# A searched order for the first stage of attention and FFN: q and k loads ahead of v, and x copied to SBUF before it is split

## The chip, the cores and the metric

One core of a Trainium2 chip runs the whole program. The metric is device time in microseconds of one launch; the median of the runs shown is 946.67 us before the change.

## What is computed

Attention with 8 heads over 8 sequences of 576 positions, then a feed-forward layer. Heads 0 to 3 see a window of 32 positions, heads 4 to 7 a window of 128 with dilation 4. Cut to what matters:

```python
scores = q @ k.T / 8            # masked: window of 32, or 128 with dilation 4
attn = softmax(scores)
x = (attn @ v)                  # heads side by side: 4608 tokens x 512
h = x @ w_in                    # 512 x 2048
out = gelu(h) @ w_out           # 2048 x 512
```

All arrays are float32. Q and K come with a larger spread than V.

## The kernel before

The 4608 tokens are cut into 16 chunks of 288 (half a sequence each). A chunk c has four pairs of heads, p = 0 and 1 for the plain window, 2 and 3 for the dilated one. This text writes S(c,p) for the scores of a pair on PE (`scores`, L310), AV(c,p) for its product with v (`av`, L395 or L411), h(c,f) for one of 16 slices of the first FFN product (`ffn_h`, L445, 12 matmuls) and o(c,f) for its part of the second (`ffn_o`, L459, 12 matmuls, 3 for each of four output slices d).

A pair goes: load of q and k (one DMA, L262) and of v (L269); S into two PSUM banks; minimum and mask on DVE (`lowest`, L322); exp on ACT (`softmax`, L331); sums, reciprocal (L352, L354); the division on DVE (L361) or, for chunks 1 and 2, on POOL (L358); a transpose on DVE (`turn`, L371); AV into PSUM (tile px, one buffer for chunks 0 and 1); and `xout`, which splits x into a high part xh (ACT, L431) and the rest xl (DVE, L434), both read from PSUM. The FFN needs x of all four pairs: each h(c,f) multiplies two parts of a weight slice with xh and one with xl. g = gelu(h) is split in the same way (L449, L452, L454).

The 32 weight slices (w_in and w_out by turns, w0 to w31) come as 64-bit words and are turned into a high and a low part on DVE and ACT (`w_rest`, `w_top`, `w_exp`, `w_high`, `w_low`). A slice is loaded once (L185), or twice, the second time shifted by two bytes (L189, tile mid_w), for the slices from TWICE[0] to TWICE[1]-1. With the second load one DVE operation (L216) stands where two stand otherwise (L220, L222).

Chunks 0 to 2 and all weights are the first stage. Its order comes from the class `Plan`: every job is a generator that tells which engine its next step takes and for how long; `run` always takes the step with the lowest key of start time and rank, and the instructions are emitted in that order. The constants ahead of the class (LATE, KAPPA, R_A and so on) are the ranks and delays. Jobs also wait in the plan for buffers (`rings`): `wo` (18 buffers: raw weights, second loads, finished w_out slices, q/k and v of chunks 0 and 1), `raw` (5 buffers: cv of the weights, and q and k from chunk 2 on), `m` (4 PSUM banks for scores and h), `px`. All loads are issued by one queue, SP, in the planned order, and a load that waits for a buffer holds all behind it. From chunk 3 on the order is a table of positions (A_SC and so on), in which attention of chunk c+1 lies between the FFN products of chunk c.

Lines that matter here: `attention_jobs` L501 to L541 adds a pair's jobs, `weight_jobs` L543 to L559 those of a weight slice, `store` L479 copies a finished output slice and writes it out (L177 on ACT or L179 on DVE).

```python
LATE, LATE_PE, COLD = 0.3, 0.3, 38
KAPPA, AHEAD = 0.00011, 6
TWICE = (1, 20)
add("load", load(s), [("begun", ("load",) + j) for j in last], [ring], delay=2.2)
```

Of the kernel before, what the change touches and what calls it, by code (L numbers as in the profile page):

```python
# [7 lines left out]
F32 = mybir.dt.float32  # L8
F32R = mybir.dt.float32r
# [8 lines left out]
P = 128  # L18
HALF = S // 2
NCH = B * 2  # L20
NPAIR = H // 2
NF = DFF // P
NC = DM // P
# [13 lines left out]

LATE, LATE_PE, COLD = 0.3, 0.3, 38  # L40
KAPPA, AHEAD = 0.00011, 6
R_ATT, R_P = (0, 680, 660), -52
R_F = 152
R_A = {"load": 172, "v": -214, "scores": 30,
       "exp": 84, "norm": 88, "t": -122, "av": -410, "x": -184, "less": -68, "sums": -20, "low": -110}
R_W, R_WL = -360, -404
R_H, R_O, R_E, R_O1 = 492, 1336, 908, 608


class Plan:  # L50
# [67 lines left out]

N_EARLY = 2

TWICE = (1, 20)


def at_once(gen):
# [10 lines left out]
def attn_ffn(ctx: ExitStack, tc: tile.TileContext, qk_p, qk_d, v_p0, v_d0, v_p, v_d, w_in, w_out, outT):  # L135
    nc = tc.nc
# [4 lines left out]
    xpool = ctx.enter_context(tc.tile_pool(name="xpool", bufs=NC))  # L141
    work = ctx.enter_context(tc.tile_pool(name="work", bufs=2))
# [150 lines left out]
    def scores(s, banks=None):  # L293

        yield {"PE": 0.75}
        if banks is None:
            s.sc = [ps_m.tile([P, 512], F32, tag="m", name="ps_sc")[:, 0:2 * KB * NU] for _ in range(2)]
        else:
            s.sc = [banks[:, h, s.p % 2 * 2 * KB * NU:(s.p % 2 + 1) * 2 * KB * NU] for h in range(2)]
        for u in range(NU):  # L300
            for r in groups(s, u):
                if s.across:
                    q0 = (4 * u + r if u < 2 else 8) * KB
                    k0 = HALF + q0
# [74 lines left out]
    def av(s, banks=None):  # L379
# [24 lines left out]
        for u in range(NU):  # L404
            b = min(KB, n - u * KB)
            for j in range(2):
                for r in sorted((r for r in groups(s, u) if r % 2 == j), reverse=s.across and s.nine > 0):
                    px, r0, _ = s.px[-1] if r >= s.px[-1][1] else s.px[0]
                    rows = slice(r // 2 * 64, r // 2 * 64 + 64)
                    for h in range(2):  # L410
                        nc.tensor.matmul(px[h * D:(h + 1) * D, r - r0, u * KB:u * KB + b],  # L411
                                         s.v[rows, u, j, h * D:(h + 1) * D], s.t[rows, 2 * u + h, j, 0:b],
                                         start=True, stop=True)

    def xout(s):
        for i, (px, r0, r1) in enumerate(s.px):
            yield {"ACT": 0.46 if len(s.px) == 1 else 0.34}
            if i == 0:
                if s.c == 1:
                    s.x = s.of["x"][:, s.p, 0], s.of["x"][:, s.p, 1]  # L420
                else:
                    s.x = tuple(xpool.tile([P, HALF], F32R, tag=n, name=n) for n in ("xh", "xl"))
            if s.across:
                two = [x[:, 0:8 * KB].rearrange("p (u r b) -> p r u b", u=2, r=4) for x in s.x]
                put = [(px[:, :, 0:2 * KB].rearrange("p r (u b) -> p r u b", u=2), two),
                       (px[:, s.nine, 2 * KB:], [x[:, 8 * KB:] for x in s.x])]
            else:
                put = [(px, [x.rearrange("p (r i) -> p r i" if s.plain else "p (i r) -> p r i", r=s.nr)[:, r0:r1]
                             for x in s.x])]
            for y, (h, l) in put:  # L430
                nc.scalar.copy(h, y)  # L431
            yield {"DVE": 0.48 if len(s.px) == 1 else 0.3}
            for y, (h, l) in put:
                nc.vector.tensor_sub(l, y, h)  # L434
# [54 lines left out]
    g0, g1, x1 = {}, {}, {}  # L489
# [11 lines left out]
    def attention_jobs(plan, c, prev, gate):  # L501

        for p in range(NPAIR):
            s, k, rank = xs[c][p], (c, p), R_ATT[c] + R_P * p

            def add(name, gen, after, take=(), give=(), delay=0.15):
                plan.add((name,) + k, gen, after, take, give, rank + R_A[name], delay)
            last, ring = [] if prev is None else [prev], "wo" if c < 2 else "raw"
            add("load", load(s), [("begun", ("load",) + j) for j in last], [ring], delay=2.2)
            v = ("v",) + k if c < 2 else ("v", c)  # L510
            if c < 2:
                add("v", load_v(s), [("begun", ("load",) + k)] + [("begun", ("v",) + j) for j in last], [ring], delay=2.2)
# [12 lines left out]
            add("scores", scores(s), [("load",) + k] + [("scores",) + j for j in last], ["m", "m"], [ring], 1.5)
            chained("low", NU, lowest, lambda b: [("scores",) + k] + ([("begun", ("t", 1, NPAIR - 1))] if c == 2 else []),
                    ["sm"], ["m", "m"])
            if c < 2:
                chained("exp", NU, softmax, lambda b: [all_of("low", NU)[0] if b == NU - 1 else ("low", b) + k] + gate)
                add("norm", norm(s), all_of("exp", NU))  # L530
            else:
                add("less", less(s), all_of("low", NU))
                add("exp", wide(s), [("less",) + k] + gate)
                add("sums", sums(s), [("exp",) + k])
                add("norm", norm(s), [("sums",) + k])
            add("t", turn(s), [("norm",) + k], ["sm"], ["sm"])
            own = ["px"] if c < 2 else ["m", "m"]
            add("av", av(s), [("t",) + k, v], own, ["sm"] + ([ring] if c < 2 else []), 1.5 if c < 2 else 0.3)
            add("x", xout(s), [("av",) + k] + ([("x1",)] if c == 1 else [("h", 0, NF - 1)] if c == 2 else []), give=own)
            prev = k  # L540
        return prev  # L541

    def weight_jobs(plan, i):  # L543

        s, f = {"twice": TWICE[0] <= i < TWICE[1]}, i // 2
        dst, src = (wouts, w_out) if i % 2 else (wins, w_in)
        rank = R_W + R_F * f + R_O * (i % 2)
        own = ["wo"] if i % 2 else []
# [21 lines left out]
    def take_o():  # L570
        yield {"": 0.0}
        pools["o"] = upper_banks("ps_o", NC)
    plan.add(("banks",), take_o(), [("x", c, p) for c in range(2) for p in range(NPAIR)], [], ["o"] * NC, -100)
    ps0, ps1 = [], {}
    for f in range(NF):
        rank = R_W + R_F * f
        for c, gs in ((0, g0), (1, g1)):
# [29 lines left out]
    steps, banks = [], {}  # L607
# [26 lines left out]
    at = 0  # L634
# [96 lines left out]
```

## Time and profile before

| | |
|---|---|
| runs | 945.33, 946.67, 946.92 us; median 946.67 |
| the profiled execution | 945.82 us, of it the span of the instructions 944.0 us |
| PE matmuls busy | 916.4 us (97%), 11632 instructions |
| PE weight loads busy | 898.6 us (95%) |
| DVE busy | 500.2 us (53%) |
| ACT busy | 435.4 us (46%) |
| POOL busy | 21.0 us (2%) |
| DMA | 83.69 MB, mean 89 GB/s; in the first tenth of the span 261 to 405 GB/s |
| chain that ended last | PE 96%, DMA 1%, issue 1%, DVE 1% |

The profiled execution took 1.8 us beside its span and lies 0.85 us under the median of the runs. PE is busy in all of the 40 slices but the first two and the last. A float32 matmul of the scores or of AV runs as two instructions, so 18 of them stand as x36 in the trace; an h or o matmul is one.

### The profile page before, as it was taken

Reading aid. Unit: us, or ns where it says so; the run is one execution under the profiler, and the core shown is the slowest. Engines: PE = TensorE matmul, PEld = TensorE weight load, DVE = VectorE, ACT = ScalarE, POOL = GpSimd, SP = SyncE. Lnnn points to the kernel's source line nnn. Section 1 sums busy time; section 2 is a strip of 40 time slices with the busy share of each in tenths; the row PEclk is TensorE's granted clock in tenths of the full one; section 3 lists DMA queues with packets and bytes.
Section 4 is the critical chain, followed back from the end, with each engine's and each line's share of the span. In section 5 each row is a group of like instructions: output and inputs, shape, how many; then the busy total and the mean of one; then the engine's idle time right before and its main releaser. Section 6 shows DMA issues by size and latency. Waiting matters only on the chain.

```text
span 944.0 us, 27638 instructions
## 1 busy us (share of the span) xinstructions
PE 916.4 (97%) x11632; PEld 898.6 (95%) x11632; DVE 500.2 (53%) x1957; ACT 435.4 (46%) x1398; POOL 21.0 (2%) x64
## 2 busy tenths in 40 slices
PE   4599999999999999999999999999999999999998
PEld 3499999999999999999999999999999999999998
DVE  6889974364635446354454635446354454635420
ACT  5535453634536245363634546255363634546240
POOL 1400020000000000000000000000000000000000
PEclk9999999999999999999999999999999999999999
DMA  9987233022040401204022040401204022040000
GB/s 319 405 297 261 92 126 137 4 78 75 8 145 8 132 17 51 103 8 145 2 82 71 8 146 8 138 9 60 93 8 145 2 86 68 13 139 8 21 1 26
DMA packets 34988, 83.69 MB, mean 89 GB/s; under 512 B 3888, under 2 KB 12080, under 8 KB 34864
## 3 DMA queue, kind: packets, MB, share of 16 engines
q1 hardware_dynamic: 34864, 81.93, 25.3%
q8 instruction: 91, 1.49, 0.7%
q14 instruction: 33, 0.27, 0.1%
HBM read 72.47 MB, written 9.44 MB: 87 GB/s over the span
## 4 chain that ended last, share of the span: by engine, by line
PE 96%; DMA 1%; issue 1%; DVE 1%; ACT 0%; SPq 0%
PE ps_h L445 44%; PE ps_o L459 44%; PE px_a L411 4%; PE ps_a L310 3%; DMA raw_qk<-qk_d 1%; PE px L395 1%; PE ps_sc L310 1%; DMA raw_w<-w_in 0%; DVE sm L322 0%; PE px L411 0%; DVE cv L199 0%; DVE sm L361 0%; ACT sm L331 0%; DVE cv L197 0%; DVE win L232 0%
## 5 line engine op out<-in xcount | busy, mean ns | idle before, releaser
L459 PE MATMUL ps_o<-g,wout 128*128 128x288 f32 x3072 | 420.1, 296 | 0.0
L459 PEld LDWEIGHTS ps_o<-g,wout 128*128 128x128 f32 x3072 | 409.7, 188 | 0.9
L445 PE MATMUL ps_h<-xh,win 128*128 128x288 f32 x1920 | 388.7, 297 | 0.0
L445 PEld LDWEIGHTS ps_h<-xh,win 128*128 128x128 f32 x1920 | 308.2, 188 | 2.8
L445 PE MATMUL ps_h<-xl,win 128*128 128x288 f32 x960 | 284.0, 296 | 0.0
L454 DVE TENSOR_TENSOR g<-gf,g 128x288 fp32r<-128x288 f32 x256 | 117.0, 457 | 259.2 <-ACT g L452 259.0
L449 ACT ACTIVATE gf<-ps_h 128x288 f32<-128x288 f32 x256 | 105.2, 411 | 297.6 <-PE ps_h L445 297.5
L445 PEld LDWEIGHTS ps_h<-xl,win 128*128 128x128 f32 x960 | 181.0, 189 | 0.0
L331 ACT ACTIVATE sm<-sm,st 128x64 f32<-128x64 f32 (+1 forms) x360 | 120.2, 335 | 12.5 <-DVE st L322 11.4
L452 ACT CAST g<-gf 128x288 fp32r<-128x288 f32 x256 | 111.0, 434 | 7.9
L431 ACT CAST xh<-px_a 128x256 fp32r<-128x256 f32 (+1 forms) x78 | 29.5, 413 | 132.7 <-PE px_a L411 84.8
L376 DVE STREAM_TRANSPOSE turned<-sm 32x192 f32<-32x192 f32 (+2 forms) x248 | 81.3, 328 | 6.2
L179 DVE COPY o_sb<-ps_o 128x288 f32<-128x288 f32 x58 | 26.4, 456 | 83.3 <-PE ps_o L459 82.4
L331 ACT ACTIVATION_READ_ACCUMULATOR sm<-sm,st 128x1 f32 (+1 forms) x360 | 67.2, 187 | 0.0
L434 DVE TENSOR_TENSOR xl<-px_a,xh 128x256 fp32r<-128x256 f32 (+1 forms) x78 | 31.3, 429 | 37.5 <-ACT xh L431 37.1
L322 DVE CUSTOM_DVE_ANT_0 sm<-ps_a,masks 128x64 f32<-128x64 f32 (+1 forms) x312 | 48.0, 216 | 0.6
L371 DVE STREAM_TRANSPOSE turned<-sm 128x256 f32<-128x256 f32 (+2 forms) x90 | 41.1, 457 | 9.0 <-POOL sm L358 4.2
L411 PEld LDWEIGHTS px_a<-turned,v_all 64*64 64x64 f32 x2184 | 35.6, 135 | 4.3 <-issue 4.3
L411 PE MATMUL px_a<-turned,v_all 64*64 64x32 f32 (+1 forms) x2184 | 38.2, 216 | 0.0
L361 DVE TENSOR_TENSOR sm<-sm,st 128x256 f32<-128x256 f32 (+2 forms) x82 | 35.1, 428 | 2.8
L352 DVE TENSOR_SCALAR st<-st 128x4 f32<-128x4 f32 (+2 forms) x90 | 14.2, 160 | 31.0 <-ACT sm L331 30.1
L310 PE MATMUL ps_sc<-raw_qk 64*32 64x64 f32 x504 | 12.3, 294 | 18.8 <-issue 8.4
(40 smaller groups left out, 392.8 us busy)
## 6 DMA issues: line engine op xcount, KB each, us to landing
raw_qk<-qk_d SPq DMA_DIRECT2D x32, 364.0 KB, 5.4
v_all<-v_p SPq DMA_DIRECT2D x28, 384.0 KB, 3.8
v_all<-v_d SPq DMA_DIRECT2D x28, 384.0 KB, 5.4
raw_qk<-qk_p SPq DMA_DIRECT2D x32, 304.0 KB, 4.2
outT<-o_sb SPq DMA_DIRECT2D x64, 144.0 KB, 1.8
raw_w<-w_in SPq DMA_DIRECT2D x16, 512.0 KB, 6.1
raw_w<-w_out SPq DMA_DIRECT2D x16, 512.0 KB, 5.7
mid_w<-w_out SPq DMA_DIRECT2D x10, 511.5 KB, 8.0
```

Of the source, the lines that this page charges most:

```text
L310: nc.tensor.matmul(s.sc[h][32 * r:32 * r + 32, u * 2 * KB:(u + 1) * 2 * KB], x[:, q0:q0 + 32], x[:, k0:k0 + 2 * KB], start=True, stop=True)
L322: nc.vector.tensor_tensor_reduce(out=s.sm[rs, i], in0=s.sc[h][rs, cols], in1=mask_of(s, u), scale=-SCALE, scalar=3.0e38, op0=ALU.add, op1= ...
L331: nc.scalar.activation(t, t, AF.Exp, bias=s.st[rs, 0, i:i + 1], scale=-1.0, accum_out=s.st[rs, 1, i:i + 1])
L361: nc.vector.tensor_mul(t, t, st.unsqueeze(2).broadcast_to((rs.stop - rs.start, 2 * (u1 - u0), 2 * KB)))
L371: nc.vector.transpose(s.t[rs, i].rearrange("p i j b -> p (i j b)"), s.sm[rs, i].rearrange("p i k -> p (i k)"))
L376: nc.vector.transpose(s.t[32 * to:32 * to + 32, i, r % 2], s.sm[32 * r:32 * r + 32, i, j * KB:(j + 1) * KB])
L411: nc.tensor.matmul(px[h * D:(h + 1) * D, r - r0, u * KB:u * KB + b], s.v[rows, u, j, h * D:(h + 1) * D], s.t[rows, 2 * u + h, j, 0:b], sta ...
L445: nc.tensor.matmul(ps, wins[f][:, t, cc * P:(cc + 1) * P], xx, start=(n == 0), stop=(n == 3 * NC - 1))
L449: nc.scalar.activation(gf, ps, AF.Gelu)
L452: nc.scalar.copy(g[:, 0], gf)
L454: nc.vector.tensor_sub(g[:, 1], gf, g[:, 0])
L459: nc.tensor.matmul(ps, wouts[f][:, t, d * P:(d + 1) * P], gs[f][:, u], start=(f == 0 and n == 0), stop=(f == NF - 1 and n == 2))
```

## The change

Three things, all in the first stage. (1) The constants of the plan are others. (2) The load of q and k of pair number n of chunks 0 and 1 may begin once the scores of pair n-5 have begun (NEXT), and no longer in step with v; those of chunk 2 wait for the low part of weight slice 1 (LATER). (3) For chunks 0 and 1 (VIA) x is copied by ACT from PSUM to an SBUF tile x32 (`xcopy`), and `xsplit` makes xh from it on ACT and xl on DVE; px is free after the copy. TWICE ends at 28 in place of 20, so slices 20 to 27 are loaded twice too.

```diff
-LATE, LATE_PE, COLD = 0.3, 0.3, 38
-KAPPA, AHEAD = 0.00011, 6
+LATE, LATE_PE, COLD = 0.4, 0.55, 38
+KAPPA, AHEAD = 6.4e-05, 6
...
+NEXT, LATER = 5, 1
+
+VIA = (0, 1)
+
-TWICE = (1, 20)
+TWICE = (1, 28)
...
+    def xcopy(s):
+        yield {"ACT": 0.46}
+        s.x32 = work.tile([P, HALF], F32, tag="go", name="x32", bufs=3)
+        nc.scalar.copy(by_group(s, s.x32, 0, s.nr), s.px[0][0])
+
+    def xsplit(s):
+        yield {"ACT": 0.34}
+        new_x(s)
+        nc.scalar.copy(s.x[0], s.x32)
+        yield {"DVE": 0.37}
+        nc.vector.tensor_sub(s.x[1], s.x32, s.x[0])
...
-            add("load", load(s), [("begun", ("load",) + j) for j in last], [ring], delay=2.2)
+            gates, at = [], NPAIR * c + p - NEXT
+            if c == 2:
+                gates = [("wlow", LATER)]
+            elif at >= 0:
+                gates = [("begun", ("scores", at // NPAIR, at % NPAIR))]
+            add("load", load(s), [("begun", ("load",) + j) for j in last] + gates, [ring], delay=2.2)
...
-            add("x", xout(s), [("av",) + k] + ([("x1",)] if c == 1 else [("h", 0, NF - 1)] if c == 2 else []), give=own)
+            if c in VIA:
+                add("xc", xcopy(s), [("av",) + k], ["go"], own)
+                add("x", xsplit(s), [("xc",) + k] + ([("x1",)] if c == 1 else []), give=["go"])
+            else:
+                add("x", xout(s), [("av",) + k] + ([("x1",)] if c == 1 else [("h", 0, NF - 1)] if c == 2 else []), give=own)
```

What the new constants do to the order is seen in the built programs. First PE, from the scores S(1,2) to the first h. L310 and L314 are scores, L395 and L399 AV, L445 and L466 h; a scores row holds 18 or 24 matmuls for each pair, an AV three rows for each pair. Before:

```order
13 L310 MATMUL ps_sc<-raw_qk 32x64 x48
14 L395 MATMUL px<-turned,v_sb 64x64 x8
15 L395 MATMUL px<-turned,v_sb 64x32 x16
16 L395 MATMUL px<-turned,v_sb 64x64 x8
17 L310 MATMUL ps_sc<-raw_qk 32x64 x18
18 L395 MATMUL px<-turned,v_sb 64x64 x6
19 L395 MATMUL px<-turned,v_sb 64x32 x12
20 L395 MATMUL px<-turned,v_sb 64x64 x6
21 L445 MATMUL ps_h<-xh,win_116 128x288 x2
```

And now:

```order
13 L314 MATMUL ps_sc<-raw_qk 32x64 x24
14 L399 MATMUL px<-turned,v_sb 64x64 x8
15 L399 MATMUL px<-turned,v_sb 64x32 x16
16 L399 MATMUL px<-turned,v_sb 64x64 x8
17 L314 MATMUL ps_sc<-raw_qk 32x64 x24
18 L399 MATMUL px<-turned,v_sb 64x64 x6
19 L399 MATMUL px<-turned,v_sb 64x32 x12
20 L399 MATMUL px<-turned,v_sb 64x64 x6
21 L314 MATMUL ps_sc<-raw_qk 32x64 x18
22 L399 MATMUL px<-turned,v_sb 64x64 x6
23 L399 MATMUL px<-turned,v_sb 64x32 x12
24 L399 MATMUL px<-turned,v_sb 64x64 x6
```

Before, S(1,2) and S(1,3) stand together, then AV(0,2), S(2,0), AV(1,1) and h(0,0). Now AV(0,2) stands between the two scores, and AV(1,0), S(2,0) and AV(1,1) follow; h(0,0) comes right behind, one AV later than before. Behind it stood AV(1,2), S(2,1), h(0,1), AV(1,3), S(2,2), h(0,2), AV(1,0), S(2,3), h(0,3); now AV(1,2), S(2,1), AV(1,3), h(0,1), S(2,2), o(0,0), h(1,0), S(2,3), h(0,2).

Second, SP, from its first row. Before:

```order
1 L262 DMA raw_qk<-qk_p 128x608
2 L185 DMA raw_w<-w_in 128x1024
3 L269 DMA v_sb<-v_p 96x512
4 L262 DMA raw_qk<-qk_p 128x608
5 L269 DMA v_sb<-v_p 96x512
6 L262 DMA raw_qk<-qk_d 128x728
7 L269 DMA v_sb<-v_d 128x512
8 L262 DMA raw_qk<-qk_d 128x728
```

And now:

```order
1 L266 DMA raw_qk<-qk_p 128x608
2 L189 DMA raw_w<-w_in 128x1024
3 L266 DMA raw_qk<-qk_p 128x608
4 L266 DMA raw_qk<-qk_d 128x728 x2
5 L273 DMA v_sb<-v_p 96x512 x2
6 L273 DMA v_sb<-v_d 128x512 x2
7 L189 DMA raw_w<-w_out 128x1024
8 L266 DMA raw_qk<-qk_p 128x608 x2
9 L266 DMA raw_qk<-qk_d 128x728 x2
```

The four q/k loads of chunk 0 now stand ahead of its v, and those of chunk 1 behind one weight. Further down SP, at the q/k loads of chunk 2, with the semaphores that each row waits for, now:

```order
25 L189 DMA raw_w<-w_out 128x1024 [waits DMAHW2_49,PE_49]
26 L266 DMA raw_qk<-qk_p 128x608 [waits DMAHW3_49,Activation_49]
27 L266 DMA raw_qk<-qk_d 128x728 [waits DMAHW4_49,DVE_49,Activation_49]
28 L266 DMA raw_qk<-qk_d 128x728 [waits DMAHW5_49,DMAHW0_49,PE_49]
29 L193 DMA mid_w<-w_out 128x2046 [waits DMAHW6_49]
```

Row 28 is the load for S(2,3). It takes the `raw` buffer of pair (2,0) and so waits for PE, for S(2,0); the second load of w5 and all later weights stand behind it. Before, the same load waited for DVE and ACT alone.

Third, DVE, at the end of the first stage, the last two rows of xl of chunk 2. Before, the last is followed by the g of chunk 2:

```order
405 L434 TENSOR_TENSOR xl<-px_2352,xh 128x192
406 L434 TENSOR_TENSOR xl<-px_2353,xh 128x96
407 L434 TENSOR_TENSOR xl<-px_2385,xh 128x192
408 L434 TENSOR_TENSOR xl<-px_2386,xh 128x96
409 L454 TENSOR_TENSOR g<-gf,g 128x288 x4
```

And now:

```order
399 L455 TENSOR_TENSOR xl<-px_2388,xh 128x96
400 L455 TENSOR_TENSOR xl<-px_2428,xh 128x192
401 L183 COPY o_sb<-ps_o 128x288
402 L455 TENSOR_TENSOR xl<-px_2429,xh 128x96
403 L475 TENSOR_TENSOR g<-gf,g 128x288 x4
```

The copy of chunk 1's last output slice (d = 3) now stands between the two halves of xl of pair (2,0). That output slice is complete with the last o matmul ahead of h(2,0), and h(2,0) reads xl of pair (2,0) with its third matmul. On PE, 12 o matmuls stand between AV(2,0) and h(2,0) where 30 stood.

## Rows read from the trace of the kernel before

**Rows 1.** Sums by stretch: us, busy us (instructions) of each engine, PE clock, DMA share, GB/s.
```profile
0.00:56.00 56.00, 31.70 (x1010) 26.62 (x1011) 43.30 (x227) 30.45 (x122) 14.09 (x40) 0.97 0.97 361
56.00:130.00 74.00, 74.00 (x559) 74.00 (x558) 72.40 (x162) 35.63 (x80) 0.00 (x0) 1.00 0.51 172
...
155.00:940.00 785.00, 785.00 (x9739) 773.34 (x9738) 370.19 (x1527) 361.03 (x1178) 0.00 (x0) 1.00 0.19 61
```
**Rows 2.** What PE waited for, 0 to 60 us: total, times, longest.
```profile
PE ps_sc L310 <- issue: 8.4, 5, 3.0
...
PE px L395 <- issue: 1.0, 2, 0.5
```
**Rows 3.** Timeline of PE, 12 to 60 us: start, length, instruction, count, idle before.
```profile
15.88 0.86 PE L310 MATMUL ps_sc<-raw_qk 64*32 64x64 f32 x32 [1.30 <-issue]
...
22.79 1.19 PE L395 MATMUL px<-turned,v_sb 32*64 32x64 f32 x53 [0.50 <-issue]
23.91 0.97 PE L310 MATMUL ps_sc<-raw_qk 64*32 64x64 f32 x48
25.38 0.78 PE L310 MATMUL ps_sc<-raw_qk 64*32 64x64 f32 x26 [0.50 <-DMA raw_qk<-qk_d]
28.91 0.64 PE L310 MATMUL ps_sc<-raw_qk 64*32 64x64 f32 x22 [2.76 <-issue]
...
35.02 1.13 PE L395 MATMUL px<-turned,v_sb 32*64 32x64 f32 x44 [0.45 <-issue]
...
41.10 0.53 PE L310 MATMUL ps_sc<-raw_qk 64*32 64x64 f32 x28 [0.97 <-issue]
...
47.58 0.43 PE L310 MATMUL ps_sc<-raw_qk 64*32 64x64 f32 x25 [2.97 <-issue]
...
52.78 0.31 PE L310 MATMUL ps_sc<-raw_qk 64*32 64x64 f32 x5 [0.37 <-issue]
```
**Rows 4.** DMA queues, 24 to 52 us: packets, MB, share of 16 engines.
```profile
q1 hardware_dynamic: 3299, 11.16, 100.8%
q8 instruction: 5, 0.08, 1.2%
```
**Rows 5.** DMA issues, 0 to 13 us: KB each, median us to landing.
```profile
raw_qk<-qk_p SPq DMA_DIRECT2D x4, 304.0 KB, 6.6
...
v_sb<-v_p SPq DMA_DIRECT2D x4, 192.0 KB, 6.7
raw_qk<-qk_d SPq DMA_DIRECT2D x2, 364.0 KB, 6.3
```
**Rows 6.** Timeline of PE, 0 to 12 us.
```profile
7.50 0.88 PE L310 MATMUL ps_sc<-raw_qk 64*32 64x64 f32 x36 [3.06 <-DMA raw_qk<-qk_p]
9.13 1.07 PE L310 MATMUL ps_sc<-raw_qk 64*32 64x64 f32 x48 [0.74 <-DVE st L352]
```
**Rows 7.** Chain that ended last, 34 to 62 us: start, us, what.
```profile
36.15 2.89 PE ps_h L445 x12
...
48.01 2.49 PE ps_h L445 x12
...
59.66 1.59 PE ps_h L445 x12
```
**Rows 8.** Timeline of DVE, end of the first stage, 150 to 155 us.
```profile
150.86 0.52 DVE L434 TENSOR_TENSOR xl<-px,xh 128x192 fp32r<-128x192 f32 x2 [1.02 <-ACT xh L431]
```
**Rows 9.** Costliest groups of the page: count, busy us, mean ns of one, idle before.
```profile
L431 ACT CAST xh<-px_a 128x256 fp32r<-128x256 f32 (+1 forms) x78 | 29.5, 413 | 132.7 <-PE px_a L411 84.8
...
L179 DVE COPY o_sb<-ps_o 128x288 f32<-128x288 f32 x58 | 26.4, 456 | 83.3 <-PE ps_o L459 82.4
```
**Rows 10.** DVE groups by line, 0 to 130 us.
```profile
L222 DVE SCALAR_TENSOR_TENSOR raw_w<-raw_w 128x512 uint32<-128x512 uint32 x13 | 8.8, 683 | 0.0
```
**Rows 11.** Timeline, 108 to 110 us: low part of w23, and o(0,11) that reads it.
```profile
108.33 0.69 DVE L232 SCALAR_TENSOR_TENSOR wout<-raw_w 128x512 fp32r<-128x512 uint32 x1
...
109.67 0.56 PE L459 MATMUL ps_o<-g,wout 128*128 128x288 f32 x3
```

More of the change, by code (lines that the diff above doesn't have):

```diff
@@ L35 @@
 EPS = 1e-9
-LATE, LATE_PE, COLD = 0.3, 0.3, 38
-KAPPA, AHEAD = 0.00011, 6
[L42 to L47, printed above, removed]
+LATE, LATE_PE, COLD = 0.4, 0.55, 38
+KAPPA, AHEAD = 6.4e-05, 6
+R_ATT, R_P = (0, 580, 1050), -748
+R_F = 12
+R_A = {"load": 236, "v": -218, "scores": 26,
+       "exp": 192, "norm": 112, "t": -46, "av": -426, "xc": -368, "x": -176, "less": -36, "sums": -4, "low": -106}
+R_W, R_WL = -508, -272
+R_H, R_O, R_E, R_O1 = 596, 1136, 644, 908
 class Plan:
@@ L413, in av, with new_x, by_group @@
                                          start=True, stop=True)
+    def new_x(s):
+        if s.c == 1:
+            s.x = s.of["x"][:, s.p, 0], s.of["x"][:, s.p, 1]
+        else:
+            s.x = tuple(xpool.tile([P, HALF], F32R, tag=n, name=n) for n in ("xh", "xl"))
+    def by_group(s, x, r0, r1):
+        return x.rearrange("p (r i) -> p r i" if s.plain else "p (i r) -> p r i", r=s.nr)[:, r0:r1]
+    def xcopy(s):
[8 more added lines that the diff above has]
+        nc.vector.tensor_sub(s.x[1], s.x32, s.x[0])
     def xout(s):
@@ L418, in xout @@
             if i == 0:
[L419 to L422, printed above, removed]
+                new_x(s)
             if s.across:
@@ L427, in xout @@
             else:
-                put = [(px, [x.rearrange("p (r i) -> p r i" if s.plain else "p (i r) -> p r i", r=s.nr)[:, r0:r1]
-                             for x in s.x])]
+                put = [(px, [by_group(s, x, r0, r1) for x in s.x])]
             for y, (h, l) in put:
@@ L538, in attention_jobs @@
             add("av", av(s), [("t",) + k, v], own, ["sm"] + ([ring] if c < 2 else []), 1.5 if c < 2 else 0.3)
[L539 removed]
+            if c in VIA:
+                add("xc", xcopy(s), [("av",) + k], ["go"], own)
+                add("x", xsplit(s), [("xc",) + k] + ([("x1",)] if c == 1 else []), give=["go"])
+            else:
+                add("x", xout(s), [("av",) + k] + ([("x1",)] if c == 1 else [("h", 0, NF - 1)] if c == 2 else []), give=own)
             prev = k
@@ L572, in take_o @@
         pools["o"] = upper_banks("ps_o", NC)
-    plan.add(("banks",), take_o(), [("x", c, p) for c in range(2) for p in range(NPAIR)], [], ["o"] * NC, -100)
+    plan.add(("banks",), take_o(), [("xc" if c in VIA else "x", c, p) for c in range(2) for p in range(NPAIR)], [],
+             ["o"] * NC, -100)
     ps0, ps1 = [], {}
```

## The prediction
> **What bounds the kernel now.** I read the sums by stretch first [rows 1]. From 56 to 940 us PE has no idle time; of its first 56 us it works 31.7, so all that an order of the first stage can win is in the 24.3 us of idle PE there, and in matmuls that run slowly after an idle stretch. The same matmuls are issued before and after. Every microsecond by which PE comes earlier out of that stretch, and stays busy, is a microsecond of the total.
>
> Then what PE waits for in it [rows 2]: 9.4 us in seven waits are put down to "issue", PE waiting for nothing that the profile shows. The timeline tells what they are [rows 3]. PE resumes after them at 15.88, 22.79, 28.91, 35.02, 41.10, 47.58 and 52.78 us. Between 22.79 and 28.91 stand 53 + 48 + 26 = 127 matmuls, and the other stretches hold 126 to 128 too, whatever they are. Each pause ends a block of instructions: the queue named instruction moved 5 packets and 0.08 MB from 24 to 52 us, 16 KB each, while the data queue held all 16 DMA engines [rows 4]. The resumes lie 6.9, 6.1, 6.1, 6.1, 6.5 and 5.2 us apart, nearly the same however much PE has to do between them. I read this so: a block is asked for when PE enters the one before it, and takes about 6.1 us to come while the loads fill the DMA engines. Waits for data in that stretch (x, px, transposes) mostly lie beneath this. By the same reading the block whose end opens at 15.88 was asked for 127 matmuls earlier, at the 94th of the 220 that stood in the first blocks: the 22nd of the second pass through S(0,2), which starts at 9.13 [rows 6], so at about 9.6 us, 6.3 us before.
>
> [...]
>
> **The change, term by term** (h(c,f), o(c,f), S and AV as above).
>
> 1. q and k first. S(0,2) needs the third q/k load. Before, S(0,1) starts at 7.50 when the q/k of its pair lands, and S(0,2) at 9.13, 192 + 364 = 556 KB of loads later [rows 5, 6]: 341 KB per us. Now no v stands ahead of these loads: the second q/k comes 192 KB sooner than it did, and the third 364 KB behind it, so the third lands 364 - 192 = 172 KB, 0.5 us, after 7.50: at 8.0 us. S(0,2) starts 1.1 us earlier, PE passes its 94th matmul at 8.5, and the block that opened at 15.88 opens at 8.5 + 6.3 = 14.8. PE is there by then: AV(0,0) ends at about 13.6 by DVE's order.
>
> 2. Three more blocks at the 6.1 us of four of the six intervals: 20.9, 27.0, 33.1 (before 22.79, 28.91, 35.02). The 6.9 after 15.88 stood once, with v loads in the queue that have now moved; I keep it for the range, as the 5.2 at the end, where the loads thin out.
>
> 3. The block ends inside AV(1,0). Its last matmuls take 0.2, S(2,0) 0.9, AV(1,1) 1.2: h(0,0) starts at 35.4 (before 36.15) and takes the 2.9 of the first h of the trace [rows 7], where a later one takes 1.59. It stands again behind an idle stretch. 24 matmuls into AV(1,2) the next block begins, at 38.6. It was asked for at 33.1. Before, this boundary cost 0.97 [rows 3]. Now the loads stand still there (term 5), so the fetch meets an empty queue; a stall of between 0 and 6.1 - 5.5 = 0.6 us. I take 0.
>
> 4. The block after that is asked for at 38.6, with the queue full again, and opens at 38.6 + 6.1 = 44.7 (before 47.58). PE reaches the boundary inside AV(1,3) at about 41.0 and stands 3.7 us. Then 0.2 for the rest, 2.5 for h(0,1) behind the pause as at 48.01 [rows 7], 1.1 for S(2,2), 1.6 each for o(0,0) and h(1,0), 1.1 for S(2,3): 52.8. The boundary in S(2,3) was asked for at 44.7 and opens by 50.8, so it costs nothing. Before, the last five matmuls of S(2,3) end at 52.78 + 0.31 = 53.1 [rows 3], with h(0,0), h(0,1) and h(0,2) done; now four such pieces are done, one more, worth 1.59. PE is ahead by 53.1 - 52.8 + 1.6 = **1.9 us**.
>
> 5. What moves past SP. The q/k load of S(2,3), and every weight from the second half of w5 on, stand behind S(2,0), which ends at 34.2; the loads ahead of it, 10.8 MB by the order, take 30 us at the 361 KB per us of the first 56 us [rows 1], from about 3 us on, and have landed by about 33. So the queue runs empty until 34.2. By its order and the durations of its operations DVE comes to w5 at about 40, and the load lands near 38.5: no cost. It costs something once S(2,0) ends later than about 36.
>
> 6. Eight more second loads, 8 x 511.5 KB, 4.2 MB, at the 11.16 MB that a full queue moved in 28 us [rows 4] 10 us of DMA time, between 56 and 130 us, where DMA is 51% busy [rows 1]. Each saves one DVE operation of 0.68 [rows 10], 5.5 us in all. Before, DVE was 72.4 of 74 us busy there, and the last part of w23 was done at 109.02, 0.65 before o(0,11) read it [rows 11]. PE would have run into that by coming 1.9 earlier; with 5.5 us less on DVE it doesn't. Saved time on DVE is otherwise worth nothing, as PE has no idle time there.
>
> 7. x through SBUF: eight more ACT operations of some 0.41 [rows 9], 3.3 us, in a stretch in which ACT works 30.5 of 56 [rows 1]. px comes free one DVE operation earlier. Both lie beneath the blocks: 0. Without that cover the copy would put 0.4 between AV and x of a pair.
>
> 8. The tail of the stage. The copy of the last output slice, 0.46 [rows 9], now stands on DVE ahead of the second half of xl of pair (2,0). It can start only when the last o matmul is done; xl's half takes 0.25 more [rows 8]. h(2,0) has two matmuls, 0.27, before it needs that half. PE stands 0.46 + 0.25 + 0.2 for the two hand-overs, less 0.27: **0.65 us**, once. Bounds: 0.4 and 0.9.
>
> Sum: 1.9 - 0.65 = 1.25 earlier. The profiled execution took 945.82 us, so the forecast is **944.5 us**; the median of the runs is 946.67, 0.85 above that execution, and I do not add it. About 0.2%, 1.9 us, is what a measurement of this kernel can tell from no change, so against the median 944.8 is the line: the forecast lies on it.
>
> **Rivals.**
>
> A. The last block comes quickly. The queue was empty until 34.2, and a fetch asked for at 38.6 may find few loads before it. With no wait at 41.0, h(0,1) is faster too (1.8) and S(2,3) ends 4.4 us earlier; h(1,0) then waits about 1 us for its x. For it: the 5.2 interval, when the loads thinned out [rows 3]. Against: SP issues eight loads within 4 us of S(2,0). Time: 944.5 - 3.4, about **941**.
>
> B. The blocks keep 6.5 to 6.9 us, or the first isn't earlier. Three or four intervals of 0.4 more take back 1.2 to 1.6: **946**. The order of the first stage changes, and PE leaves it at the same time, since the instructions come no faster.
>
> C. Slower: the load queue behind S(2,0). If the blocks or AV(1,0) put S(2,0) later than 36 us, each microsecond of it makes w5 and all later weights a microsecond late, and DVE with them. By the durations of DVE's operations the tightest weight, w9, is ready some 4.7 us before o(0,4) reads it; beyond an S(2,0) at about 40.5 PE waits. At 43.5 that is 3 us lost and the gain of 1.9 gone as well: **949**. For it: SP holds everything behind one row. Against: four blocks would have to take 2.5 us more each.
>
> D. The fetches are hidden, as they are from 56 us on. Then only data bounds the stage: DVE has some 23.5 us of operations up to the transpose of pair (1,1), from 5.2 on and with 2.5 of waits, so AV(1,1) starts at 31.2, h(0,0) at 32.4 in place of 35.4, and the stall of 3.7 at 41.0 falls away: 6 us more, **939**. [...] Seven pauses of 127 matmuls speak against it.
>
> **How the numbers follow.** Forecast 0.45, A 0.2, B 0.2, C 0.1, D 0.05. A and D are faster by over 0.2%, and half of the forecast's share: 0.47. C is slower: 0.10. The rest, 0.43, is within. The range reaches from A, 941, to between B and C, 947.5: D and most of C are left out. The forecast's own range, with the bounds of terms 2, 3 and 8, is 943 to 946.
>
> **What would show it.** PE's pauses on issue should end near 14.8, 20.9, 27.0, 33.1 and 44.7, 127 matmuls apart, and h(0,0) start near 35.4. The data queue should be empty for a few us about 34. A pause of some 0.6 us should stand on PE ahead of the third matmul of h(2,0), with DVE's copy as what it waited for, and no pause between 56 us and there. The forecast is wrong if the pauses on issue lie other than 6 us apart, if PE pauses for a weight or for x(1,3) between 45 and 130 us, or if PE, which should be busy 33 to 34 of its first 56 us, is busy under 32.5 or over 35.

## The result and the profile after

The changed kernel takes 947.67 us in the median (22 runs, 946.13 to 950.38); the kernel before, run beside it, takes 945.69 (22 runs). The ratio is 1.0023, 95% interval 1.0015 to 1.0031: 2.0 us slower. The forecast was 944.5, with a range of 941.0 to 947.5: the wrong direction, and just outside.

The profiled execution took 949.89 us (span 948.1), 2.2 above its median. The runs differ by the mean clock that PE was granted: 946.13 us at 0.998 (one run), 946.9 to 948.7 at 0.996 or 0.997 (14), 949.7 to 950.4 at 0.994 (7). So the profile shows one of the longer runs, and more of one loss than the median has.

The sums by stretch, after (columns as in [rows 1]):

```profile
0.00:56.00 56.00, 31.23 (x946) 26.60 (x947) 40.66 (x213) 31.44 (x125) 14.71 (x40) 0.91 0.92 322
56.00:130.00 74.00, 73.73 (x596) 73.31 (x595) 66.40 (x158) 34.09 (x78) 0.00 (x0) 1.00 0.74 258
...
160.00:940.00 780.00, 780.00 (x9702) 768.32 (x9701) 370.36 (x1527) 361.12 (x1177) 0.00 (x0) 1.00 0.19 61
```

Behind 160 us PE has no idle time in either kernel. In the first 56 us PE was granted 0.91 of its clock, not 0.97, and was busy for 31.23 us, under the 32.5 that the prediction named as a sign against it. DVE is off the edge: 66.4 of 74 us, from 72.4.

What PE waited for in the first 56 us, after, against [rows 2]:

```profile
PE px L399 <- issue: 14.4, 4, 4.4
```

14.4 us on instructions in four waits, where 9.4 in seven stood. The timeline of PE, against [rows 3] and [rows 7]:

```profile
14.98 1.14 PE L314 MATMUL ps_sc<-raw_qk 64*32 64x64 f32 x36 [1.83 <-DMA raw_qk<-qk_p]
...
22.04 1.18 PE L399 MATMUL px<-turned,v_sb 32*64 32x64 f32 x53 [3.23 <-issue]
...
28.45 0.92 PE L399 MATMUL px<-turned,v_sb 32*64 32x32 f32 x38 [3.74 <-issue]
...
34.32 0.48 PE L399 MATMUL px<-turned,v_sb 32*64 32x64 f32 x7 [3.00 <-issue]
...
36.66 0.85 PE L466 MATMUL ps_h<-xh,win 128*128 128x288 f32 x2
...
39.52 0.91 PE L399 MATMUL px<-turned,v_sb 32*64 32x64 f32 x64
40.37 0.91 PE L314 MATMUL ps_sc<-raw_qk 64*32 64x64 f32 x36
41.32 0.81 PE L399 MATMUL px<-turned,v_sb 32*64 32x64 f32 x52
46.57 0.51 PE L399 MATMUL px<-turned,v_sb 32*64 32x64 f32 x12 [4.44 <-issue]
47.00 0.85 PE L466 MATMUL ps_h<-xh,win 128*128 128x288 f32 x2
...
50.18 0.42 PE L314 MATMUL ps_sc<-raw_qk 64*32 64x64 f32 x2
...
51.63 3.25 PE L480 MATMUL ps_o<-g,wout 128*128 128x288 f32 x12
54.68 2.41 PE L466 MATMUL ps_h<-x,win 128*128 128x288 f32 x12
57.01 0.30 PE L314 MATMUL ps_sc<-raw_qk 64*32 64x64 f32 x2
...
58.22 0.53 PE L466 MATMUL ps_h<-xh,win 128*128 128x288 f32 x2
```

The pauses stand at the instructions that were foretold, 127 matmuls apart, and end 1.1 to 1.9 us later than foretold; the boundary inside AV(1,2) cost nothing, as foretold. But the last pause, inside AV(1,3), took 4.44 us, and what follows is slow: o(0,0) holds PE for 3.05 us (51.63 to 54.68) and h(1,0) for 2.33, where 1.6 each was reckoned. The granted clock says why. After:

```profile
42.00:46.00 4.00, 0.13 (x10) 0.00 (x0) 3.97 (x19) 0.00 (x0) 0.00 (x0) 0.99 1.01 400
46.00:56.00 10.00, 9.28 (x90) 8.48 (x91) 7.31 (x32) 2.90 (x6) 0.00 (x0) 0.50 1.03 410
```

And before:

```profile
41.00:48.00 7.00, 3.93 (x153) 3.36 (x153) 7.00 (x27) 2.62 (x5) 0.00 (x0) 1.00 1.03 406
48.00:52.00 4.00, 4.00 (x95) 3.60 (x94) 2.25 (x16) 1.18 (x3) 0.00 (x0) 0.60 0.97 380
```

From 42 to 46 us PE was busy for 0.13 us, and from 46 to 56 it was granted half its clock (0.50; the clock records of the two profiles hold 1.00 and 0.50 alone): matmuls of h follow each other 0.24 us apart there (47.65 to 47.89), and 0.13 behind it (58.59 to 58.72). By the trace's clock records that stretch is 10.2 us long; before, 3.4. The records begin only at 39.08 us (before, at 38.56); the time ahead of them counts as full clock in these columns and in the mean clock of a run.

The end of the first stage, DVE and PE, after:

```profile
158.14 0.46 DVE L183 COPY o_sb<-ps_o 128x288 f32<-128x288 f32 x1 [1.11 <-PE ps_o L480]
158.51 0.25 DVE L455 TENSOR_TENSOR xl<-px,xh 128x96 fp32r<-128x96 f32 x1
```

```profile
157.94 0.42 PE L466 MATMUL ps_h<-xh,win 128*128 128x288 f32 x2
158.81 0.40 PE L466 MATMUL ps_h<-xl,win 128*128 128x288 f32 x1 [0.45 <-DVE xl L455]
...
160.24 0.42 PE L466 MATMUL ps_h<-xh,win 128*128 128x288 f32 x2
```

The copy stands ahead of xl, and PE waits. h(2,0) takes 160.24 - 157.94 = 2.30 us; the next one follows in the usual 1.6. Before, h(2,0) began at 154.50, h(2,1) at 156.08, 1.58 later:

```profile
154.50 0.43 PE L445 MATMUL ps_h<-xh,win 128*128 128x288 f32 x2
...
156.08 0.42 PE L445 MATMUL ps_h<-xh,win 128*128 128x288 f32 x2
```

So the whole difference of the two profiled spans, 948.1 - 944.0 = 4.1 us, is 157.94 - 154.50 = 3.4 in the first stage and 0.7 in its tail.

### The profile page after: what moved, and what is told of

Its sections match the earlier page's. It is cut to its first block, busy times and chain, and to the rows that moved or that the text cites. A ratio compares the mean times of both kernels' runs of the same rounds, so it can differ in the third digit from the quotient of the medians.

```text
span 948.1 us, 27660 instructions
## 1 busy us (share of the span) xinstructions
PE 919.2 (97%) x11632; PEld 901.3 (95%) x11632; DVE 496.6 (52%) x1949; ACT 437.5 (46%) x1406; POOL 21.7 (2%) x64
## 4 chain that ended last, share of the span: by engine, by line
PE 96%; issue 2%; DMA 1%; ACT 1%; DVE 0%; SPq 0%; DVEq 0%
PE ps_o L480 44%; PE ps_h L466 44%; PE px_a L415 4%; PE ps_a L314 3%; DMA raw_qk<-qk_p 1%; PE px L399 1%; PE ps_sc L314 1%; PE px L415 0%; ACT sm L335 0%; ACT L470 0%; ACT gf L470 0%; DVE o_sb L183 0%; DVE cv L203 0%; ACT win L213 0%; DVE turned L375 0%
## 5 line engine op out<-in xcount | busy, mean ns | idle before, releaser
L466 PE MATMUL ps_h<-xh,win 128*128 128x288 f32 x1920 | 389.2, 298 | 0.0
L466 PEld LDWEIGHTS ps_h<-xh,win 128*128 128x128 f32 x1920 | 308.9, 189 | 2.7
L466 PE MATMUL ps_h<-xl,win 128*128 128x288 f32 x960 | 284.5, 296 | 0.5 <-DVE xl L455 0.5
L466 PEld LDWEIGHTS ps_h<-xl,win 128*128 128x128 f32 x960 | 181.3, 189 | 0.7 <-DVE xl L455 0.7
L326 DVE DVE_READ_ACCUMULATOR2_ANT st<- 128x1 f32 (+2 forms) x384 | 30.5, 79 | 0.0
L356 DVE TENSOR_SCALAR st<-st 128x4 f32<-128x4 f32 (+2 forms) x90 | 14.4, 161 | 30.6 <-ACT sm L335 29.8
```

The lines of the kernel that those rows point to most:

```text
L326: nc.vector.tensor_tensor_reduce(out=s.sm[rs, i], in0=s.sc[h][rs, cols], in1=mask_of(s, u), scale=-SCALE, scalar=3.0e38, op0=ALU.add, op1= ...
L466: nc.tensor.matmul(ps, wins[f][:, t, cc * P:(cc + 1) * P], xx, start=(n == 0), stop=(n == 3 * NC - 1))
```

## The experiments

Three theories. **1:** instruction blocks come late behind the loads, a complete pause is followed by the half clock, and the tail costs 0.7. **2:** the blocks alone; the slow matmuls have another cause. **3:** late loads or DVE set the pace. For the runs the order that the plan chose was written out as a list; MOVES puts a step of one job (job, step) ahead of a step of another. Medians of the kernel before differ by up to 0.9 us between the groups of runs (945.69 to 946.59), so ratios to it are compared; the change itself has 1.0023.

### PE kept busy in the pause

```diff
             s.px = [(px[:, 0:s.nr, 0:n], 0, s.nr)]
+            if (s.c, s.p) == (1, 3):
+                for _ in range(20):
+                    nc.tensor.matmul(px[:, 0, 128:128 + HALF], wins[0][:, 0, 0:P], xs[0][0].x[0],
+                                     start=True, stop=True)
```

> The changed kernel with 20 extra matmuls of 128x288 ahead of AV(1,3), into columns of its bank that nothing reads: nothing of the work moves, PE is only kept busy in what was the pause (41.3 to 46.6). Theory 1: the pause on issue shrinks to 0.5 to 2.6 us and ends near 46.6 as before; no half clock behind it, or a short one; h(0,1) takes 1.6 to 1.8 and not 3.2, o(0,0) and h(1,0) 1.6 each; S(2,3) ends near 54.3, 4 us earlier than in the changed kernel's profile, though PE has more to do: 946 profiled. Theory 2 (blocks alone): no change, S(2,3) at 58.3, 949.9 profiled, the half clock for some 10 us. Theory 3 (loads, DVE): no change either.

945.72 us (10 runs), ratio 0.9990 [0.9980, 0.9999]: more work, and 0.33% faster than the change. The granted clock was 1.000 in seven of the ten runs and 0.998 in three, against 0.998 at most in the change. The profiled run is one of the three; its timeline:

```profile
41.37 2.90 PE L437 MATMUL px<-xh,win 128*128 128x288 f32 x20
44.20 0.46 PE L448 MATMUL px<-turned,v_sb 32*64 32x64 f32 x32
47.48 0.49 PE L448 MATMUL px<-turned,v_sb 32*64 32x32 f32 x32 [2.82 <-issue]
47.90 0.54 PE L515 MATMUL ps_h<-xh,win 128*128 128x288 f32 x2
...
51.24 2.30 PE L529 MATMUL ps_o<-g,wout 128*128 128x288 f32 x12
53.38 1.78 PE L515 MATMUL ps_h<-x,win 128*128 128x288 f32 x12
...
55.74 0.53 PE L515 MATMUL ps_h<-xh,win 128*128 128x288 f32 x2
```

The block came 0.9 us later than in the change's profile (47.48 against 46.57), and h(0,2) still started 2.5 us earlier (55.74 against 58.22): from the end of the pause the same work, and 20 instructions of AV more, took 8.3 us, not 11.65. Theories 2 and 3 expected no change. The profiled run took 1.3 us more than theory 1 had for it: the block came 0.9 later, and 3.4 us of half clock are left in it, so that o(0,0) took 2.14 us and not 1.6. A mean clock of 1.000 alone would not prove much, since the time ahead of the first record counts as full; but the seven runs with it took 944.6 to 946.0 us, and the three at 0.998 took 947.0 to 948.7.

### The same with the tail mended

```diff
-MOVES = []
+MOVES = [("x.2.0", 3, "store.1.3", 0)]
```

> The changed kernel with two of the single edits together: the 20 extra matmuls ahead of AV(1,3) and the last copy behind xl. If the half clock after the pause and the tail are what the change lost, their gains add: the extra matmuls gave 1.95 us in the medians, the tail takes 0.7 us by the traces (65 matmuls from the 1885th on take 7.83 us with the wait and 7.11 without), so 945.0 median, under the kernel before by 0.5 to 1.2 us. Rival (something else of the change costs as well, spread over the stage): 946 or more.

945.18 us (12 runs, 943.29 to 947.12), ratio 0.9983 [0.9973, 0.9994]; the kernel before beside it 946.39. The forecast was 945.0, the rival's 946 or more. At a granted clock of 0.999 or 1.000 six runs took 943.3 to 945.0, at 0.998 six took 945.4 to 947.1. By the ratios that is 3.8 us under the change, more than the 2.0 that it lost: without these two losses it is 1.2 us ahead of the kernel before by the medians. (The kernel before has its own half clock, 3.4 us in its profile, and no extra matmuls against it.) In the run with the extra matmuls alone nothing but activity was added, and the mean clock, 0.996 or 0.997 in 14 of the change's 22 runs, was 1.000 in seven of ten.

### The tail alone

The move of the run above, without the extra matmuls.

> The changed kernel with the copy of the last output slice behind the second half of xl of pair (2,0) on DVE, instead of ahead of it. Theory 1: the wait of 0.45 us that PE has ahead of the third matmul of h(2,0) falls to 0.1 or less, nothing else changes, and the median goes from 947.7 to 947.2. Rival: DVE cannot be ready earlier, since xl's half waits for its bank's other reader or for ACT; then the wait stays at 0.3 or more.

947.51 us (10 runs), ratio 1.0005 [0.9996, 1.0014], just clear of the change's 1.0015 to 1.0031. By the ratios that is 1.7 us less, where 0.5 was expected; but none of these runs has a mean clock of 0.994, and seven of the change's 22 have, so that the times do not price the tail. The trace does: the wait is gone, and h(2,0) runs as before, 1.59 us from its start to that of h(2,1).

```profile
156.24 0.42 PE L511 MATMUL ps_h<-xh,win 128*128 128x288 f32 x2
156.50 0.29 PE L511 MATMUL ps_h<-xl,win 128*128 128x288 f32 x1
...
157.83 0.42 PE L511 MATMUL ps_h<-xh,win 128*128 128x288 f32 x2
```

This profile shows something else as well. Up to the tail PE's instructions are those of the change, but by the clock records the half clock lasts 6.8 us (44.2 to 51.0) and not 10.2:

```profile
47.22 0.51 PE L444 MATMUL px<-turned,v_sb 32*64 32x64 f32 x12 [4.01 <-issue]
...
56.65 0.53 PE L511 MATMUL ps_h<-xh,win 128*128 128x288 f32 x2
```

From the end of the pause to h(0,2) PE takes 9.4 us, where it took 11.65 in the change's profile: 2.2 us apart for the same instructions, with the clock as the one difference that the profiles show.

### Real work in the pause

```diff
-MOVES = []
+MOVES = [("h.0.1", 0, "scores.2.1", 0)]
```

> The changed kernel with one matmul job moved: h(0,1), 12 matmuls, now ahead of S(2,1) instead of behind AV(1,3). Theory 1 (a complete pause of PE inside AV(1,3), waiting for its instruction block, and after it a stretch at the half clock): h(0,1) runs from 40.4 in what was the pause, S(2,1) waits until 42.7 for DVE to free its banks, and the pause on issue shrinks from 4.4 us to about 2.0, ending again near 46.6, since the block is asked for at the same place. The granted clock stays full, or falls for about as long as in the kernel before (3.4 us, not 10.2), so that S(2,3) ends at 52.5 to 53.5 in place of 58.3: a profiled time of 944.5 to 945.5 against 949.9. Theory 2 (the blocks alone, the slow matmuls have another cause): only the 3.25 us of h(0,1) leave the path, S(2,3) ends at 55.0, 946.6 profiled, and the half clock still lasts some 10 us. Theory 3 (late loads or DVE set the pace, not the blocks): whatever PE does earlier it waits for later, 949 to 950.

947.71 us (10 runs), ratio 1.0011 [1.0002, 1.0020], profiled 947.92: not what theory 1 said. The pause shrank to 2.8 us and ended at 46.77, as expected; two things were not. PE, 36 us on:

```profile
PE px L444 <- issue: 2.8, 1, 2.8
PE ps_sc L359 <- ACT gf L515: 1.5, 2, 1.2
```

S(2,2) needs the bank of h(0,1), whose gelu stood on ACT behind x(1,3): 1.2 us. And the half clock came all the same:

```profile
47.00:54.00 7.00, 5.78 (x90) 5.25 (x83) 6.54 (x26) 2.78 (x6) 0.00 (x0) 0.53 1.03 409
```

It lasts 6.8 us by the records, in place of 10.2. Half a pause filled is not enough. The length of the pause does not settle it either: the profile with 20 extra matmuls has the same 2.8 us and half as long a half clock behind it (3.4 us). What decides that stays open. h(0,2) starts at 56.15, 2.1 us earlier than in the change's profile.

### Fewer loads ahead of the blocks

```diff
-        s, f = {"twice": TWICE[0] <= i < TWICE[1]}, i // 2
+        s, f = {"i": i, "twice": 6 <= i < TWICE[1]}, i // 2
```

> The changed kernel with the second loads of w1 to w5 left out (5 x 511.5 KB, some 7 us of the data queue in its first 34 us); DVE builds the shifted words itself, one operation of 0.68 more for each of the five. The order is otherwise the same. Theory 1 (a block's fetch stands behind the loads in the DMA engines): the data queue runs empty near 27 and not 34, the fetch that is asked for at about 28.4 starts some 1.1 us after it was asked for, as the one at 34.3 did, and not 3.6 us after, so that its block opens by 32.5 instead of 34.3, and the blocks ahead of it lie under 6.4 us apart. How much of that reaches the time hangs on DVE, which has 3.4 us more to do by then: 945 to 948. Rival (a fetch takes 6 us whatever else moves): the starts stay 3.6 to 4.5 us behind the asking, the resumes 5.9 to 7 us apart, and the time is 948 to 950.

945.93 us (10 runs), ratio 0.9994 [0.9985, 1.0003]. PE's pauses:

```profile
22.70 1.19 PE L445 MATMUL px<-turned,v_sb 32*64 32x64 f32 x53 [4.06 <-issue]
...
28.02 0.93 PE L445 MATMUL px<-turned,v_sb 32*64 32x32 f32 x38 [2.64 <-issue]
...
31.96 0.49 PE L445 MATMUL px<-turned,v_sb 32*64 32x64 f32 x7 [1.07 <-issue]
```

They lie 5.3 and 3.9 us apart where the change has 6.4 and 5.9, as theory 1 said; its rival had 5.9 to 7. (The profiled run is the slowest of the ten, 946.88: its clock records begin only at 52.93 us, and until then its h matmuls follow each other 0.24 us apart, the pace of the half clock, under a mean clock of 0.999.) PE enters a block at 28.02; the queues show loads nearly at an end (28.1 to 29.4 us, first line) and the next block's packet right behind (29.4 to 30.7, second):

```profile
q1 hardware_dynamic: 5, 0.01, 1.8%
...
q8 instruction: 1, 0.02, 5.3%
```

It starts at 29.52, 1.5 us after 28.02. In the change PE enters at 28.45, the loads fill the engines until 31.9, and the packet starts at 32.03, 3.6 us after; from 34.32 on, with the queue empty, it starts at 35.45, 1.1 after. The change's queues, 28.5 to 31.9 us, where no instruction packet stands, and 32 to 33.2:

```profile
q1 hardware_dynamic: 461, 1.38, 101.9%
...
q8 instruction: 1, 0.02, 5.8%
```

So, as I read it, a fetch is asked for when PE enters a block and stands behind the loads: its packet starts 1.1 us after with the queue empty and 3.6 with it full. In the change PE's waits on issue come to 14.4 us.

### Two parts undone

x split from PSUM again (`VIA = ()`):

> One part of the change undone alone: x of the first two halves is split from PSUM again, without the copy in SBUF (eight ACT operations fewer, 3.3 us of ACT in the first 50 us; px comes free one DVE operation later). Order otherwise the same. Theory 1: both lie beneath the blocks; the pauses on issue stay within 0.5 us of where they were (22.0, 28.5, 34.3, 46.6), no change of the time over 0.3 us: 947 to 948.5 by the luck of the half clock. Rival: the copy costs 0.4 us between AV(1,3) and h(1,0) or holds px, and its removal gives 0.4 to 1 us: 946.5 to 947.2.

948.92 us (10 runs), ratio 1.0030 [1.0021, 1.0039]: 0.7 us over the change by the ratios, intervals overlapping. Neither expectation was right. PE now waits for DVE's reading of px, which the copy had taken away:

```profile
PE px L446 <- DVE x L502: 3.5, 3, 2.0
```

h(0,1) starts at 47.90, against 47.00, so most of these 3.5 us lie beneath the blocks; how much reaches the end stays open. Four of the seven waits on issue now stand at the first matmul of an AV (17.10, 20.83, 27.20, 33.58 us) and not 127 matmuls apart; what they wait for the trace does not name. The three runs at a mean clock of 1.000 took 948.7 to 950.2 us, so that this loss is not one that the mean clock shows.

w20 to w27 loaded once (`1 <= i < 20`):

> Another part undone alone: the eight additional second loads (w20 to w27). DVE gets its 5.5 us back between 56 and 130 us, 72 of 74 us busy again. Theory 1: what the change lost was lost before 58 us, so that these loads neither cost nor give anything by themselves; PE has no wait between 58 and 130 or one under 0.5 us, 947.5 to 948.5. Rival A (the saved DVE time is what keeps the later weights in time): PE waits 1 to 3 us for w23, w25 or w27, 948.5 to 950.5. Rival B (the additional 4.2 MB disturb PE): 0.5 us or more faster, 947 or less.

951.20 us (5 runs), ratio 1.0042 [1.0028, 1.0055]; the interval overlaps the change's, so that the trace must decide. Rival A was right in kind: in 60 to 165 us PE waits for a weight, which it does not do in the change.

```profile
PE ps_h L512 <- DVE win L282: 1.2, 1, 1.2
```

PE goes on at 127.98 us. The slice is w28, the 15th of w_in, and not w23, w25 or w27; the time lies above rival A's 948.5 to 950.5. DVE's 5.5 us were no cushion: by this order the later weights need them, even with PE 3 us late.

### Towards a faster kernel

```diff
-MOVES = []
+MOVES = [("h.0.0", 0, "t.1.1", 0), ("av.1.0", 0, "t.1.1", 0), ("h.0.1", 0, "av.1.2", 0), ("x.2.0", 3, "store.1.3", 0)]
```

The first two put h(0,0) ahead of AV(1,0).

> Three moves together: h(0,0) ahead of AV(1,0), into the pause that ends at 34.3; h(0,1) ahead of AV(1,2); the tail of e2. Theory 1: h(0,0) runs from 30.3 to 33.1, the pause in AV(1,0) falls from 3.0 us to 0.5 or less and ends at 34.3 as before, S(2,0) ends at 35.7, AV(1,1) at 36.9, h(0,1) by 39, S(2,1) near 43.6 (behind DVE's release of the banks of S(2,0)), the pause in AV(1,3) is 2 us or less and ends at 45 to 46.6, S(2,3) ends at 51 to 52.5, and the half clock lasts at most as long as before. That is 3 to 4 us ahead of the kernel before for the same work done: 942 to 943. Theory 2 (blocks without a clock): 944 to 945. Theory 3 (loads and DVE set the pace): 946 to 948, with new waits for x, w or px in place of those on issue.

945.00 us (11 runs), ratio 0.9981 [0.9972, 0.9990], faster than before, but 2 to 3 us over theory 1's forecast. It is theory 2's number (944 to 945), but not for theory 2's reason, since the clock did fall. The pause in AV(1,0) fell to 1.0, that in AV(1,3) stayed at 3.5 us (h(0,1) had left it), S(2,1) and S(2,2) waited 1.3 and 1.2 us for gelus on ACT, and the clock was 0.55 from 41 to 52 us. Next (eight moves, twelve steps), with the gelus earlier, h(0,2) in the pause and the q/k load of S(1,0) ahead of w1:

```diff
+         ("h.0.0", 1, "xc.1.0", 0), ("h.0.0", 2, "xc.1.0", 0), ("h.0.1", 1, "xc.1.2", 0), ("h.0.1", 2, "x.1.2", 0),
+         ("h.0.2", 0, "av.1.3", 0), ("h.0.2", 1, "xc.1.3", 0), ("h.0.2", 2, "xc.1.3", 0), ("load.1.0", 0, "wload.1", 0)]
```

> The three moves of the run with h(0,0), h(0,1) and the tail, and besides: both gelu and cast of h(0,0) and h(0,1) earlier on ACT (their banks held up S(2,1) 1.3 us and S(2,2) 1.2 us), h(0,2) ahead of AV(1,3) as work for the pause that is left there, and the q/k load of S(1,0) ahead of w1. Theory 1 (blocks are asked for when PE enters the one before; a pause with little work behind it is followed by the half clock): S(1,0) starts by 13.5 and not 14.6 to 15, each later block opens 1 to 1.5 us earlier (20.7, 27, 33, 44); the pause in AV(1,3) is under 1.5 us, no half clock or at most the 3.4 us of before, S(2,3) ends at 50 to 51.5 with h(0,2) done as well: 940 to 942. Theory 2 (blocks alone): 942 to 944. Theory 3 (DVE's weights are the next bound): PE waits for w4 to w9 between 45 and 75 and the time stays at 943.5 to 945.

942.18 us (5 runs), ratio 0.9955 [0.9943, 0.9968], at the border of theory 1 (940 to 942) and theory 2 (942 to 944): the time does not tell them apart. PE's pauses:

```profile
14.60 0.86 PE L361 MATMUL ps_sc<-raw_qk 64*32 64x64 f32 x32 [0.72 <-issue]
...
21.11 1.19 PE L446 MATMUL px<-turned,v_sb 32*64 32x64 f32 x53 [2.78 <-issue]
...
45.59 0.66 PE L446 MATMUL px<-turned,v_sb 32*64 32x32 f32 x37 [2.37 <-issue]
```

S(1,0) starts at 13.45 now, and its block holds it at 14.60: earlier data gained 0.4 us there. The blocks between open at 28.07 and 34.62. All four from 21.11 on open 0.4 to 1.6 us later than theory 1 said. The clock still fell (0.72 from 46 to 52 us, and for 3.4 us from 36.6 on). Three more on this kernel: 12 extra matmuls as in the first run, w1 to w5 loaded once, and both.

> The eight-move kernel (h(0,0), h(0,1) and h(0,2) in the pauses, earlier gelu, S(1,0)'s load earlier, tail) with 12 extra matmuls of 128x288 ahead of AV(1,3), which keep PE busy in the 2.4 us that are left of the pause; their results are not read. Theory 1: no half clock behind the pause (47 to 51 in the kernel without them), o(0,0) takes 1.8 and not 3.25, S(2,3) ends near 51.3; 940.5 to 941.3. Theory 2 (the half clock has another cause, such as the pause in AV(0,2)): 942 to 942.5.

> The eight-move kernel with w1 to w5 loaded once each. Theory 1 (fetches stand behind loads): the blocks that open at 28.1 and 34.6 come at 26.5 to 27.5 and 30.5 to 32; h(0,0) is then ahead of its block by data alone, S(2,0) ends 2 us earlier, the pause in AV(1,3) ends at 42.5 to 44 in place of 45.6: 940 to 941.5. Rival (3.4 us more of DVE in the first 40 us hold up turn(1,1) to turn(1,3) and w4): new waits of PE for turned or win, 942 to 943.

> Both edits of the two runs before together. Theory 1: the gains add where both exist, 939 to 940.5. Rival: once the blocks come earlier, DVE's weights are the bound, and the extra matmuls only delay: 941 to 942.5.

They took 942.35, 941.13 and 942.14 us; ratios 0.9949 [0.9936, 0.9962], 0.9938 [0.9926, 0.9951], 0.9945 [0.9932, 0.9958]. By its time only the second came out as its theory 1 said; the first and the third lie where their rivals were. With the extra matmuls the pause in AV(1,3) was gone and the mean clock was 1.000 in four of five runs (in the profile it does not fall behind the first record, at 41.66 us), yet the time did not fall: they take some 1.7 us themselves (an estimate from the 2.90 us of 20), and a new wait came, for DVE's low part of g:

```profile
PE ps_o L531 <- DVE g L526: 1.1, 2, 0.9
```

With fewer loads PE waits 2.2 us for DVE ahead of h(0,2), and the clock fell for 10.2 us from 39.5 on. I take DVE for the next bound; no run with less work on DVE shows it. The fastest, 941.13, is 0.62% under the kernel before; the intervals of all four kernels overlap, so that they cannot be told apart.

## Why the prediction was wrong

What bounds the stage was read rightly: blocks of 127 matmuls that come 5.9 to 7.1 us after PE enters the one before. By its terms:

1. q and k first. S(0,2) started at 7.45 (8.0 predicted). PE passed the first boundary at 14.98 (14.8), though not for the block: S(1,0)'s own q/k landed last. With that load earlier the block itself opened at 14.60.
2. Three blocks at 6.1 each: they took 7.06, 6.41 and 5.87. The last opened at 34.32 where 33.1 was said. In [rows 3] only three of the six intervals are 6.1, not four.
3. h(0,0) took 2.9 and the boundary in AV(1,2) nothing, as said; both 1.2 us later by term 2.
4. **The step that failed.** Block: 6.7 us after 39.9, open at 46.57, not 44.7; 1.9 in all with term 2. Behind it, from start to start: rest of AV 0.43 (0.2 predicted), h(0,1) 3.18 (2.5), S(2,2) 1.45 (1.1), o(0,0) 3.05 (1.6), h(1,0) 2.33 (1.6), S(2,3) 1.21 (1.1): 11.65 in place of 8.1, 3.5 lost. So the late blocks took the whole gain of 1.9, and the slow work behind the pause turned it into a loss of 3.4 in the profiled run (3.5 by this sum). That the clock is the cause is shown twice: with PE kept busy in the pause this stretch took 8.3 us, and with the same instructions but a shorter half clock 9.4. I had taken only the first h after a pause as slow, from [rows 7], and asked for no cause; the clock of 0.97 in [rows 1] was the cause in sight. A change that turns seven pauses into four longer ones had its half clock more often: one of its 22 runs has a mean clock of 0.998 or more, against 38 of the 72 runs of the kernel before that were taken beside the experiments. That had no term and no rival.
5. The load queue behind S(2,0) was empty from 33.7 to 36.7, as S(2,0) ended at 35.6; PE waited for no weight. No cost: right.
6. The additional second loads: hidden, and DVE's time was needed. Right; 1.2 us of waits come without them.
7. x via SBUF: no cost. Right; the px waits it takes away were not counted.
8. The tail: 0.65 predicted, 0.7 measured, by the mechanism named. The 0.2 for the two hand-overs in it was an estimate that no row shows; they took 0.04 us (the last o matmul's end at 158.10 to the copy at 158.14) and 0.05 (xl's end at 158.76 to 158.81).

Rival B (blocks of 6.5 us) named what took the gain, and was priced at 946; rival C had the sign but not the mechanism; A and D fell with the pauses.

In the medians the loss is 2.0 us: 0.7 is the tail, and the rest is less than what PE kept busy in the pause gives back (0.33%, 3.1 us by the ratios). The longer half clock of a run at 0.994 cost 2.2 us against one at 0.996, by the two profiles above; why one run got 0.994 and another 0.998 stays open.

## What to carry to other kernels

Price an order by what PE does after a pause, not by the pause alone: in the profiled run a pause of 4.4 us with nothing on PE cost another 3.5 us behind it, at half the clock. Where a trace waits on "issue", count the instructions between the waits: where the count was constant here (127), the wait was for the next block, and it moved with the loads in flight; where it was not, as with x split from PSUM, four waits were for something else, which the trace does not name. And read the last instructions of a stage in the planned order: one copy ahead of one operand cost 0.7 us.

## What was not expected of the hardware

- Twenty matmuls whose results nobody reads made the kernel faster, 0.9990 against 1.0023 of the kernel before.
- A block's fetch started 1.1 to 1.5 us after PE entered the block before with the data queue empty, and 3.6 to 4.5 us after with it full (19.53 behind 14.98, 26.08 behind 22.04, 32.03 behind 28.45).
- h(0,0)'s matmuls follow each other 0.24 us apart from 37.06 to 38.98, and 0.13 at its end, while the clock column shows 1.00 for the whole time (36 to 40 us). The clock records begin at 39.08, where the distance changes, and the column shows 1.00 where there is no record. In the kernel before they begin at 38.56, in the run with w1 to w5 loaded once at 52.93. The distance between matmuls shows such a stretch; the column does not.
- The extra time of the tail was more than the idle time shown: 0.45 us of wait, 0.7 us from h(2,0) to h(2,1).
